# One score product per step in the last third of a fused routing-attention and feed-forward kernel, with the stores of set-aside sums issued a step later

## The chip, the cores and the metric

The kernel runs on one core of one Trainium2 chip. The metric is device time in microseconds (us) of one launch, the median of several executions. A core has five engines that run at the same time and wait for one another through semaphores: PE (matrix products), DVE (vector work), ACT (activations and copies), POOL (more vector work, and some DMA issues) and SP, which here does nothing but issue DMAs. Each engine takes its instructions strictly in program order, so an instruction that waits holds back everything behind it on that engine.

## The reference

Routing attention with 4 batches, 8 heads, 768 tokens and 64 dimensions per head, then a feed-forward block on the (3072 x 512) result:

```
q_assign = argmax(q_n @ c_n.T)            # 16 clusters, per head; k_assign likewise
mask     = q_assign[..., :, None] == k_assign[..., None, :]
scores   = where(mask, scale * q @ k.T, -1e9)
attn     = softmax(scores)                # rows, with + 1e-9 in the sum
x        = concat of heads of attn @ v    # (3072, 512)
h = x @ w_in                              # (3072, 2048)
g = h - tanh(h)
out = g @ w_out                           # (3072, 512)
```

All inputs and the output are float32.

## The kernel before

**Steps.** Attention is worked through in 96 steps. A step is one (pair of heads `n`, half of the queries `half`, third of the keys `s`): it has 2 blocks of 128 keys, 2 heads and 384 queries. There are 16 pairs, 4 for each batch; `HALF` is 12 and `NS` is 3, so the last third of the list is steps 72 to 95 with the pairs 12 to 15 (batch 3). For each step

- `begin` issues the score products (tile `sc`, line 544): 4 matmuls that contract over 64 rows, each head in its own half of PE's rows. ACT then takes the exponential in place (line 566).
- `select` multiplies by the routing mask: 4 DVE instructions (line 576) that compare a row of query codes (`row`, brought from DRAM tensor `q_codes` by `spread`, line 499) with the key's code and write the weights `e`. POOL adds the weights up (`sum`, lines 588 and 592).
- `value` multiplies weights and values (tile `av`, line 601): 4 matmuls that contract over all 128 rows.

The scores of a step are made one step ahead of its values. The weight tiles `e` have two buffers, the score tiles `sc` two, the PSUM tiles of tag `f` three.

**Fills.** Between the products of a step PE is given products of the feed-forward block of the batch before. These come as a list `fill`, whose items each carry a weight; `whole` is the sum of the weights, and step by step items are taken until the share of the weight that is due is spent. For batch 2, which is worked in steps 72 to 95, the list is 56 up products (`pu`, weight 1.3 each) and then 14 down products (`pd`, line 1302): 7 products by Strassen's scheme for each of two blocks of 128 tokens. The function `weight` gives the down products their weights. Each item calls `between`, which issues a slice of the step's other work (`todo`: masks, routing, transposes, checks, stores).

**Runs.** In some steps (where `runs(at)` is true) the kernel does a *run*: it issues the score products of the next three steps one after another, with products of the fill between them, and these are then written in a form that contracts over 64 rows like the scores (`three_in_rows` for the up products, the argument `rows_` for the down products). A down product in this form needs two PSUM tiles, and DVE adds both (two instructions in place of one). The values of the three steps follow later.

**Set-aside blocks.** The third block of 128 tokens of batch 2 (`ASIDE`) is not multiplied in this fill: its seven left operands, and for each the sum of its two halves, are stored to DRAM (`aside`) and multiplied in the tail with batch 3. `set_aside` issues the store of the operand (line 1265), has DVE make the sum into a tile `u` (line 1269; the pool has two buffers), and issues the store of the sum (line 1272). The calls are put on a list, `behind`, which is emptied into `todo` only in a step that is no run and is not followed by one:

```
if not run and not runs(at + 1):
    todo += behind
    behind.clear()
```

With a run in every third step, that is one step in three. All the stores here, the load of `row`, the loads of the factors (`w_in`, line 928) and the loads of weights to be checked (`again`, line 1765) go through SP's queue. Each load of `row` comes after the store of the codes (`q_codes`, line 479), whose source DVE makes (lines 475 and 477).

Of the kernel before, what the change touches and what calls it, by code (L numbers as in the profile page):

```python
# [58 lines left out]
def kernel(  # L59
# [10 lines left out]
    nc = tc.nc  # L70
# [13 lines left out]
    HCH = NCH // 2  # L84
# [95 lines left out]
    def fast():  # L180
# [663 lines left out]
        HF = CF // 2  # L844
        CH = CD // 2
        HM = DM // 2
        HQ, HC = HF // 2, HM // 2
        PRODUCTS = (1, 2, 6, 7, 4, 5, 3)
        SLOT = {which: i for i, which in enumerate(PRODUCTS)}
# [8 lines left out]
        behind = []  # L858
        aside = dram.tile([len(ASIDE), 7, P, HF + HQ, P], F32, name="aside", bufs=1)
# [345 lines left out]
        def strassen_items(b: int):  # L1205
# [31 lines left out]
            aside_ = sum(block[0] == b for block in ASIDE)  # L1237

            def weight(i: int):

                if not aside_:
                    return 3.4
                i = i // HCH * (HCH - aside_) + i % HCH
                return 3.4 if i < 3 else 1.0 if i > 11 else 6.58

            def lower(j: int, which: int, part: int):

# [8 lines left out]
            def set_aside(which: int):  # L1256

                d = [i for i in range(len(ASIDE)) if ASIDE[i][0] == b]
                for i in d:
                    c = slice(ASIDE[i][1] * P, (ASIDE[i][1] + 1) * P)  # L1260
                    quarter_ = {
                        1: (0, 0), 2: (1, 0), 3: (1, 0), 4: (1, 1), 6: (0, 0), 7: (0, 1)
                    }.get(which)
                    t = G[:, :, quarter_[0], quarter_[1], c] if quarter_ else left1[:, :, c]
                    nc.sync.dma_start(aside[i, SLOT[which], :, 0:HF], t)
                    total_ = late_pools["u"].tile([P, 2, TB], F32, name="u")
                    total_ = total_.rearrange("p a n -> p (a n)")[:, 0 : HQ * P]
                    total_ = total_.rearrange("p (a n) -> p a n", n=P)
                    nc.vector.tensor_tensor(  # L1269
                        out=total_, in0=t[:, 0:HQ], in1=t[:, HQ:HF], op=ALU.add  # L1270
                    )
                    nc.sync.dma_start(aside[i, SLOT[which], :, HF : HF + HQ], total_)

            def lower_aside(which: int, part: int):
                for block in ASIDE:
# [3 lines left out]
            def down_product(k_: int, j: int, between, rows_=False):  # L1279
# [66 lines left out]
                if j < 2:  # L1346
                    if k_ == 2:
                        behind.append(lambda: lower_aside(6, j))
                    elif k_ == 4:
                        behind.append(lambda: lower_aside(3, j))  # L1350
                    if (k_, j) in SET_ASIDE:
                        behind.append(lambda: set_aside(SET_ASIDE[k_, j]))
# [306 lines left out]
            if b == B - 1:  # L1659
# [17 lines left out]
                return ups + deep_items()  # L1677
            return ups + [
                (weight(k_ * HCH + j), 2, lambda between, rows_=False, k_=k_, j=j: down_product(k_, j, between, rows_))
                for k_ in range(len(PRODUCTS)) for j in range(HCH) if (b, j) not in ASIDE  # L1680
            ]


        NS = NCH // 2
        HALF = HP * NS
# [161 lines left out]

        def runs(at: int):

            return at > 4 * HALF and at % NS == NS - 1 and at % (2 * HALF) < 2 * HALF - 1  # L1850

        fill, whole, spent, since, over = [], 0.0, 0.0, 0, 1
        for at, (n, half, s) in enumerate(steps):
# [18 lines left out]


            run, chunks = runs(at), []
            if run:
                coming = now + fill
                for _ in range(NS - 1):
                    size = 1 if coming[0][1] == 2 else 3
                    assert all(len(it) == 4 for it in coming[:size]) or size == 1
                    chunks.append(coming[:size])  # L1880
                    coming = coming[size:]
                first_ones = sum(len(it) for it in chunks)
                while len(now) < first_ones + 1:
                    now.append(fill.pop(0))
                    spent += now[-1][0]
                now = now[first_ones:]
            elif runs(at + 1):
                ups_left = sum(len(it) == 4 for it in fill)
                if ups_left < 3 * (NS - 1):
                    for _ in range(ups_left % 3):  # L1890
                        now.append(fill.pop(0))
                        spent += now[-1][0]
# [122 lines left out]
# [3 lines that stand above are left out]
# [317 lines left out]
```

## Time and profile before

| | |
|---|---|
| median of 3 runs | 938.41 us (936.21 to 941.18) |
| profiled execution | 933.44 us |
| its span, first to last instruction | 931.6 us |
| mean granted TensorE clock | 0.995 |
| PE busy | 911.1 us, 98% of the span |
| DVE, POOL, ACT busy | 690.9, 523.6, 295.2 us |
| end of the steps, first product of the tail | 765.35 us after the start |

A row of the timeline has the start in us, how long the merged instructions took, the engine, the source line, the operation, the tile written and the tiles read, the shape and the count; in brackets, how long the engine had been idle before it and which instruction released it. Each float32 matmul shows as two records, so a step's scores are "x8". In a matmul's shape `64*128` means that it contracts over 64 rows, `128*64` that it contracts over 128 rows and makes 64 columns; two such matmuls run side by side. SPq is SP's queue of DMA issues.

### The profile page before, as it was taken

How to read it: one execution, taken by the hardware profiler on the slowest of the kernel's cores; microseconds unless marked ns; L12 is line 12 of the kernel's file. 1: busy time of each engine (PE TensorE's matmuls, PEld its weight loads, DVE VectorE, ACT ScalarE, POOL GpSimd, SP SyncE). 2: the span in 40 equal slices, each digit the busy share in tenths (PEclk: the TensorE clock that was granted, in tenths of full speed). 3: DMA queues.
4: the chain of work that ended last, by engine and by line, in shares of the span. 5: the costliest groups of instructions: out<-in, count | busy, mean ns of one | idle time of the engine just before them, and what ended most of it. 6: DMA issues, size and time to landing. Idle time of an engine off the chain costs nothing.

```text
span 931.6 us, 18750 instructions
## 1 busy us (share of the span) xinstructions
PE 911.1 (98%) x7286; PEld 513.0 (55%) x7286; DVE 690.9 (74%) x1288; ACT 295.2 (32%) x466; POOL 523.6 (56%) x403
## 2 busy tenths in 40 slices
PE   8999999999999999999999999999996999999997
PEld 4434433356653454444666654455563744449997
DVE  7779777986799598666675678766666567867995
ACT  5676653233332323333322213333421211211000
POOL 0236533568878566888664644977773755682000
PEclk9999999999999999999999999999998999999999
DMA  7777584794437974485494666466475446533532
GB/s 170 232 206 182 162 179 130 221 265 135 95 95 238 279 259 117 135 180 183 125 226 149 164 190 149 148 184 166 118 246 178 152 132 190 174 115 139 204 104 84
DMA packets 187439, 158.37 MB, mean 170 GB/s; under 512 B 119200, under 2 KB 161744, under 8 KB 184144
## 3 DMA queue, kind: packets, MB, share of 16 engines
q1 hardware_dynamic: 177696, 134.40, 51.7%
q0 software_dynamic: 6048, 20.98, 6.8%
q10 hardware_dynamic: 3600, 1.74, 0.7%
q8 instruction: 59, 0.97, 0.4%
q14 instruction: 36, 0.29, 0.1%
HBM read 130.33 MB, written 26.75 MB: 169 GB/s over the span
## 4 chain that ended last, share of the span: by engine, by line
PE 87%; DVE 5%; DMA 3%; ACT 1%; issue 1%; POOL 1%; SPq 1%; DVEq 0%; ACTq 0%; POOLq 0%
PE pu L1021 20%; PE sc L544 14%; PE av L601 13%; PE pd L1302 12%; PE pp L1520 9%; PE pu L1012 6%; PE h L787 4%; PE hd L1152 3%; PE o L803 3%; DVE e L576 2%; PE sim L405 1%; DMA row<-q_codes 1%; PE den L674 1%; DMA up_factors<-made 1%; DVE u L1269 1%
## 5 line engine op out<-in xcount | busy, mean ns | idle before, releaser
L592 POOL TENSOR_TENSOR sum<-sum,e 128x768 f32<-128x768 f32 x112 | 206.2, 1841 | 83.8 <-DVE e L576 79.2
L576 DVE SCALAR_TENSOR_TENSOR e<-row,code,sc 128x384 f32<-128x384 bf16 x336 | 183.7, 607 | 63.2 <-ACT sc L566 27.8
L566 ACT ACTIVATE sc<-sc 128x768 f32<-128x768 f32 x168 | 126.5, 793 | 196.5 <-PE sc L544 167.6
L544 PE MATMUL sc<-t,t 64*128 64x384 f32 x768 | 150.1, 506 | 6.8 <-DVE e L576 6.5
L601 PE MATMUL av<-e,vals 128*64 128x384 f32 x768 | 143.7, 494 | 0.0
L1021 PE MATMUL pu<-xT,w_in 128*64 128x384 f32 (+1 forms) x864 | 130.6, 440 | 0.0
L1215 POOL TENSOR_TENSOR G<-G,th 128x768 f32<-128x768 f32 (+1 forms) x51 | 88.0, 1747 | 43.9 <-ACT th L1213 43.8
L1302 PE MATMUL pd<-w_in,G 128*64 128x256 f32 (+1 forms) x960 | 110.5, 381 | 0.2 <-DVE c L1318 0.2
L544 PEld LDWEIGHTS sc<-t,t 64*128 64x128 f32 x768 | 70.3, 187 | 72.7 <-issue 35.8
L1302 PEld LDWEIGHTS pd<-w_in,G 128*64 128x64 f32 (+1 forms) x960 | 81.3, 158 | 30.8 <-issue 5.8
L1021 PEld LDWEIGHTS pu<-xT,w_in 128*64 128x64 f32 x864 | 61.7, 137 | 60.4 <-issue 49.4
L601 PEld LDWEIGHTS av<-e,vals 128*64 128x64 f32 x768 | 51.6, 136 | 75.8 <-issue 68.7
L588 POOL TENSOR_TENSOR sum<-e 128x768 f32<-128x768 f32 x28 | 51.8, 1851 | 72.7 <-DVE e L576 59.7
L1213 ACT ACTIVATE th<-G 128x768 f32<-128x768 f32 (+1 forms) x51 | 39.3, 805 | 109.0 <-DVE G L1006 75.3
L1021 PE MATMUL pu<-diff,w_in 128*64 128x384 f32 x400 | 71.6, 488 | 0.4 <-DVE u L1006 0.4
L803 PE MATMUL o<-w_out,g 128*64 128x512 f32 x256 | 57.4, 593 | 0.0
L1012 PE MATMUL pu<-diff,w_in 64*128 64x384 f32 x176 | 49.6, 482 | 0.0
L1021 PEld LDWEIGHTS pu<-diff,w_in 128*64 128x64 f32 x400 | 28.9, 137 | 35.3 <-issue 27.0
L1012 PE MATMUL pu<-xT,w_in 64*128 64x384 f32 x160 | 48.3, 482 | 0.0
L638 ACT COPY xT<-av 128x384 f32<-128x384 f32 x32 | 15.3, 479 | 94.8 <-PE av L601 94.7
L787 PE MATMUL h<-xT,w_in 128*64 128x384 f32 x256 | 42.8, 486 | 0.0
L1006 DVE TENSOR_TENSOR G<-pu,u 128x384 f32<-128x384 f32 x72 | 38.6, 550 | 5.2 <-PE pu L1021 3.1
(283 smaller groups left out, 1290.7 us busy)
## 6 DMA issues: line engine op xcount, KB each, us to landing
w_in<-up_factors SPq DMA_DIRECT2D x32, 896.0 KB
w_in<-down_factors SPq DMA_DIRECT2D x25, 1024.0 KB
again<-in_moe_w_in_dram SPq DMA_DIRECT2D x32, 256.0 KB
again<-in_moe_w_out_dram SPq DMA_DIRECT2D x32, 256.0 KB
vals<-in_v_dram SPq DMA_DIRECT2D x32, 192.0 KB
raw<-in_moe_w_in_dram POOLq DMA_DIRECT2D x12, 512.0 KB, 4.4
row<-q_codes SPq DMA_DIRECT2D x29, 192.0 KB
raw<-in_moe_w_out_dram POOLq DMA_DIRECT2D x10, 512.0 KB, 4.6
```

What stands on the lines that cost most here:

```text
L544: nc.tensor.matmul(sc[i][:, h, 0:TB], lhsT=turned[n, 1][r].rearrange("p a n -> p (a n)")[:, j * P : (j + 1) * P], rhs=turned[n, 0][r, half ...
L566: nc.scalar.activation(out=out, in_=sc[i][:, :, 0:TB], func=ACT.Exp, scale=SCALE)
L576: nc.vector.scalar_tensor_tensor(out=e[:, h].rearrange("p (j n) -> p j n", n=P), in0=rows[n, half][:, h], scalar=(codes[n][:, h, 1, j : j ...
L592: nc.gpsimd.tensor_tensor(out=s, in0=s, in1=pair[i], op=ALU.add)
L601: nc.tensor.matmul(avs[n, half][h * D : h * D + D], lhsT=vals[n][:, h, j], rhs=e[i][:, h], start=(j == 0), stop=(j == NCH - 1),)
L787: nc.tensor.matmul(h[r], lhsT=w_in[i][:, c, o * P : (o + 1) * P][:, r], rhs=xT[c][:, half], start=(c == 0), stop=(c == CD - 1),)
L803: nc.tensor.matmul(acc[sub][r], lhsT=gs[f % HF][:, f // HF, sub * P : (sub + 1) * P][:, r], rhs=w_out[f // FQ][:, f % FQ], start=(f == seq ...
L1012: return nc.tensor.matmul(ps, lhsT=streams[base + i][r, c, k_], rhs=right[c][r], start=start, stop=stop)
L1021: nc.tensor.matmul(ps[r], lhsT=streams[base + i][:, c, k_, r], rhs=right[c], start=(c == 0), stop=(c == CH - 1),)
L1215: nc.gpsimd.tensor_tensor(out=t, in0=t, in1=th, op=ALU.subtract)
L1302: nc.tensor.matmul(out_, lhsT=w, rhs=x, start=(i == 0), stop=(i == HF - 1))
L1520: nc.tensor.matmul(ps[r], lhsT=left[:, i, r], rhs=right[i], start=(i == 0), stop=(i == HQ - 1),)
```

## The change

Three edits. The score runs are confined to steps before 83 (`7 * HALF - 1`): the four at steps 83, 86, 89 and 92 are no longer made, so from there each step has its own scores, and down products keep their form over 128 rows. The weight of a down product of the fill with a set-aside block becomes 4.55 for all, so that the share of the list done in a step is another. And the store of a set-aside sum is put on `behind` instead of being issued at once: it goes out with the next emptying of the list.

```diff
             def weight(i: int):
 
-                if not aside_:
-                    return 3.4
-                i = i // HCH * (HCH - aside_) + i % HCH
-                return 3.4 if i < 3 else 1.0 if i > 11 else 6.58
+                return 4.55 if aside_ else 3.4
...
                     nc.vector.tensor_tensor(
                         out=total_, in0=t[:, 0:HQ], in1=t[:, HQ:HF], op=ALU.add
                     )
-                    nc.sync.dma_start(aside[i, SLOT[which], :, HF : HF + HQ], total_)
+                    behind.append(lambda total_=total_, i=i: nc.sync.dma_start(
+                        aside[i, SLOT[which], :, HF : HF + HQ], total_
+                    ))
...
         def runs(at: int):
 
-            return at > 4 * HALF and at % NS == NS - 1 and at % (2 * HALF) < 2 * HALF - 1
+            return 4 * HALF < at < 7 * HALF - 1 and at % NS == NS - 1 and at % (2 * HALF) < 2 * HALF - 1
```

The three places below are in steps 85 to 93, with the last two pairs of heads. Lines behind the second edit have other numbers in the changed kernel: the down product's 1302 is 1301 there, the set-aside lines 1265, 1269 and 1272 are 1262, 1266 and 1269.

On PE, the scores of the last pair's first three steps (`t_5743` and `t_5686` are that pair's turned keys). A first shape of 128 rows on a `pd` row is the form over 64 rows of contraction with two outputs; 64 is the form over 128. Before, one run:

```order
L674 MATMUL den<-sum,ones 32x384 x4
L544 MATMUL sc<-t_5743,t_5719 128x384 x4
L1302 MATMUL pd<-w_in_137,G 128x256 x16
L544 MATMUL sc<-t_5743,t_5719 128x384 x4
L1302 MATMUL pd<-w_in_137,G 128x256 x16
L544 MATMUL sc<-t_5743,t_5719 128x384 x4
L1302 MATMUL pd<-w_in_136,G 64x256 x16
L601 MATMUL av<-e,vals 64x384 x12
```

and now, steps 89 and 90, which make the scores of 90 and 91:

```order
L544 MATMUL sc<-t_5686,t_5678 128x384 x4
L601 MATMUL av<-e,vals 64x384 x4
L1301 MATMUL pd<-w_in_138,G 64x256 x16
L674 MATMUL den<-sum,ones 32x384 x4
L1301 MATMUL pd<-w_in_137,G 64x256 x16
L544 MATMUL sc<-t_5686,t_5678 128x384 x4
L601 MATMUL av<-e,vals 64x384 x4
L1301 MATMUL pd<-w_in_137,G 64x256 x16
```

The three scores stood together with down products in their own form between them, and three values followed in one block; now a step's scores, the values of the step before and one or two down products alternate, and PE goes from one form to the other and back in each step.

On SP, the last pair's codes and the stores of set-aside operands. Before:

```order
L479 DMA q_codes<-qc 4x32x32
L1265 DMA aside<-G 128x8x128
L1272 DMA aside<-u 128x512
L1265 DMA aside<-G 128x8x128
L1272 DMA aside<-u 128x512
L1265 DMA aside<-G 128x8x128
L1272 DMA aside<-u 128x512
L1765 DMA again<-in_q_dram 128x384 x2
L499 DMA row<-q_codes 128x768
```

and now:

```order
L479 DMA q_codes<-qc 4x32x32
L1269 DMA aside<-u 128x512 x2
L1262 DMA aside<-G 128x8x128
L499 DMA row<-q_codes 128x768
L928 DMA w_in_136<-down_factors 128x2048
L1262 DMA aside<-G 128x8x128
L1269 DMA aside<-u 128x512
```

Three pairs of stores and two loads stood between the codes and the `row` that is made of them; now two stores of sums made in the step before and one of an operand do.

On DVE, the same place. Before:

```order
L576 SCALAR_TENSOR_TENSOR e<-row,code,sc 128x384 x4
L475 CAST listed_codes<-code 128x12
L477 STREAM_TRANSPOSE qc<-listed_codes 128x32
L1269 TENSOR_TENSOR u<-G 128x512 x3
L1777 TENSOR_REDUCE largest<-again 128x1 x2
L749 TENSOR_TENSOR xT<-xT,den 128x384 x2
L1777 TENSOR_REDUCE largest<-again 128x1 x2
```

and now, in steps 87 and 88:

```order
L576 SCALAR_TENSOR_TENSOR e<-row,code,sc 128x384 x4
L475 CAST listed_codes<-code 128x12
L477 STREAM_TRANSPOSE qc<-listed_codes 128x32
L1317 SCALAR_TENSOR_TENSOR c<-pd,w_in_139 128x256
L1266 TENSOR_TENSOR u<-G 128x512
L1776 TENSOR_REDUCE largest<-again 128x1 x2
L576 SCALAR_TENSOR_TENSOR e<-row,code,sc 128x384 x4
L1266 TENSOR_TENSOR u<-G 128x512
```

Three sums stood in a row ahead of the masks of the last pair; now one stands between two steps' masks, and the two before it were made in step 86.

## The prediction

> **What bounds the kernel now.** I read the page first, for the engine that fills the span.
>
> ```profile
> span 931.6 us, 18750 instructions
> PE 911.1 (98%) x7286; PEld 513.0 (55%) x7286; DVE 690.9 (74%) x1288; ACT 295.2 (32%) x466; POOL 523.6 (56%) x403
> ...
> L592 POOL TENSOR_TENSOR sum<-sum,e 128x768 f32<-128x768 f32 x112 | 206.2, 1841 | 83.8 <-DVE e L576 79.2
> ```
>
> PE is busy 98% of the span, so the time is PE's own work plus what PE waits for. POOL's largest group, the sums of the weights, takes 1.84 us apiece and waits for DVE's masks; that matters below. Second, the waits of PE, longest first (us in total, times, longest):
>
> ```profile
> PE sc L544 <- DVE e L576: 6.5, 1, 6.5
> PE den L647 <- POOL sum L592: 1.9, 1, 1.9
> ```
>
> Both lie in the stretch that the change rewrites. Third, busy time by stretch (us from the start; length, then busy us and counts of the engines, the granted clock, DMA share, GB/s):
>
> ```profile
> 561.38:668.44 107.06, 107.06 (x682) 52.42 (x680) 76.45 (x152) 34.72 (x52) 76.86 (x50) 1.00 0.59 158
> ...
> 705.28:719.55 14.27, 6.63 (x50) 4.11 (x49) 9.01 (x14) 2.47 (x4) 5.22 (x4) 0.91 0.81 240
> 719.55:726.42 6.87, 6.87 (x41) 5.43 (x42) 4.86 (x10) 1.59 (x2) 5.75 (x4) 0.70 0.39 145
> ...
> 263.39:343.41 80.02, 80.02 (x547) 37.30 (x546) 67.49 (x99) 24.91 (x38) 57.88 (x47) 1.00 0.77 223
> ```
>
> The up products of the last third (first row) leave PE no idle time. The trouble starts with the down products, 668.44 to 765.35. Fourth, PE's timeline there:
>
> ```profile
> 700.63 4.72 PE L601 MATMUL av<-e,vals 128*64 128x384 f32 x24
> 705.28 0.84 PE L674 MATMUL den<-sum,ones 128*32 128x384 f32 x4
> 707.29 0.84 PE L674 MATMUL den<-sum,ones 128*32 128x384 f32 x4 [1.17 <-POOL sum L592]
> 708.06 1.56 PE L544 MATMUL sc<-t,t 64*128 64x384 f32 x8
> 709.45 3.62 PE L1302 MATMUL pd<-w_in,G 64*128 64x256 f32 x32
> 719.55 2.93 PE L544 MATMUL sc<-t,t 64*128 64x384 f32 x8 [6.48 <-DVE e L576]
> 722.24 4.36 PE L1302 MATMUL pd<-w_in,G 64*128 64x256 f32 x32
> 726.42 1.47 PE L544 MATMUL sc<-t,t 64*128 64x384 f32 x8
> ...
> 731.32 4.72 PE L601 MATMUL av<-e,vals 128*64 128x384 f32 x24
> 735.97 1.56 PE L544 MATMUL sc<-t,t 64*128 64x384 f32 x8
> 737.37 3.62 PE L1302 MATMUL pd<-w_in,G 64*128 64x256 f32 x32
> 740.82 1.46 PE L544 MATMUL sc<-t,t 64*128 64x384 f32 x8
> 742.11 3.62 PE L1302 MATMUL pd<-w_in,S 64*128 64x256 f32 x32
> ...
> 751.10 4.72 PE L601 MATMUL av<-e,vals 128*64 128x384 f32 x24
> 757.75 0.87 PE L647 MATMUL den<-sum,ones 128*64 128x384 f32 x4 [1.93 <-POOL sum L592]
> ```
>
> Starts tell the pace: undisturbed scores take 1.29 us (740.82 to 742.11), a down product in the scores' form 3.45 (737.37 to 740.82). Values have as many records of as many columns as scores, 1.29, so three in a row should take 3.87. Last, the chain of waits into the 6.48 us:
>
> ```profile
> 702.25 2.19 DVE e L576 x4
> 704.44 0.94 DVE listed_codes L475
> ...
> 705.62 2.17 DVE u L1269
> ...
> 707.81 2.62 DMA aside<-u
> ...
> 714.45 3.69 DMA row<-q_codes
> ...
> 718.26 1.15 DVE e L576 x2
> ...
> 719.55 2.93 PE sc L544 x8
> ```
>
> Three set-aside sums come in one lump. The third needs a buffer, so DVE waits for the first one's store (2.62 us); SP waits for each sum before it goes on; the `row` of the last pair leaves only at 714.45, lands 3.69 later, and PE's second scores wait for its masks.
>
> **The change part by part. What the runs' end removes.** Measured group by group against the pace:
> - 709.45 to 719.55 is 10.10 for a product of 3.45: 6.65.
> - After the pause the clock is 0.70 (windows): scores 2.69 (719.55 to 722.24) for 1.39, the product behind 4.18 for 3.45: 1.30 + 0.73 = 2.03.
> - `den` at 705.28 takes 2.78 to the next scores, of which the last 0.77 (707.29 to 708.06) is work that nothing hides: 2.0, the wait for POOL's last sum (its 1.17 and the lost overlap).
> - 751.10 to 757.75 is 6.65 for three values: 2.78. 0.68 of it recurs in the other two blocks: 700.63 to 705.28 and 731.32 to 735.97 are 4.65, less 3.87 and 0.10 for a change of form: 0.68 each, 1.36. The third value there waits for masks that DVE could start only once the first value had freed an `e` buffer.
>
> Together 6.65 + 2.03 + 2.0 + 2.78 + 1.36 = 14.8. In the new order no three masks are bunched, POOL adds a step's weights while PE has a product of the next, and stores of sums no longer stop SP. I count all of it as gone and price separately what comes late next. DVE's second addition for each 64-row down product (0.96 for two, below) goes too, at no gain: PE, not DVE, ends these stretches.
>
> **What it adds on PE.** Each step by itself costs changes of form. The same alternation stands in other parts of this profile:
>
> ```profile
> 263.39 1.56 PE L544 MATMUL sc<-t,t 64*128 64x384 f32 x8
> 264.88 1.51 PE L601 MATMUL av<-e,vals 128*64 128x384 f32 x8
> 266.22 3.62 PE L1152 MATMUL hd<-w_out,g 128*64 128x256 f32 x32
> 269.78 1.56 PE L544 MATMUL sc<-t,t 64*128 64x384 f32 x8
> ```
>
> Scores 1.49, values 1.34, a product of 32 records 3.56: 6.39 in all, against 1.29 + 1.29 + 3.45 = 6.03. An excursion to the scores' form and back so costs 0.35, and a run costs the same 0.35 for three steps (0.10 in, 0.10 at its first scores, 0.15 out). The order has 16 excursions between the fill's start and the tail, 8 before: 8 x 0.35 = 2.8. Bounds: 2.0 (some changes into the 32-column `den` fall away) and 3.5.
>
> [...]
>
> **The weights.** Moving products between steps is worth nothing by itself: PE's list is the same, and 561.38 to 668.44 had no wait. Its worth is that the 14 down products are spread over steps 85 to 95, two in steps 85, 89 and 93 and one in each of the others.
>
> **What is late next.** DVE, with a step of 6.39 as cover:
>
> ```profile
> 705.54 3.91 DVE L1269 TENSOR_TENSOR u<-G 128x512 f32<-128x512 f32 x2
> ...
> 711.13 1.00 DVE L1777 TENSOR_REDUCE largest<-again 128x1 f32<-128x384 f32 x2
> ...
> 712.05 1.02 DVE L749 TENSOR_TENSOR xT<-xT,den 128x384 f32<-128x384 f32 x2
> ...
> 726.62 0.96 DVE L1318 SCALAR_TENSOR_TENSOR w_in<-pd,w_in 128x256 f32<-128x256 f32 x2 [1.16 <-PE pd L1302]
> 727.33 1.50 ACT L566 ACTIVATE sc<-sc 128x768 f32<-128x768 f32 x2 [3.97 <-PE sc L544]
> ```
>
> Scores need two exponentials before the masks; from scores to the end of four masks is about 4.2 (0.9 until ACT starts, 726.42 to 727.33; one exponential, half of 1.50; 2.19 of masks; gaps). The next scores come 2.2 later. I walk the order with these rows, an estimate: step 86 leaves DVE 2.7 into step 87, step 87's masks end at 5.0, codes at 6.1. SP then issues the codes' store and the two sums' stores, and the third sum (its buffer held a step longer by the deferral) can start when the first has landed, 2.62 on: 3.1 into step 88. Sum and check end at 4.8 to 5.6, the masks behind at 7.0 to 7.8, PE wants them at 7.0: 0 to 0.8 lost. I take 0.4. The last `row` leaves SP about 2 into step 88, lands by 6, and is wanted 2 into step 89: 2 us of slack or more. At the end one down product instead of two covers the last division and differences; the PSUM tile that the tail's fifth product needs is freed about 0.5 late, and a wait of POOL for the last sum may stay: 0.3 to 1.5, I take 0.7. In the 80 us from 263.39 each step already has its own scores, like the one quoted, with DVE busy 67.49 of 80.02 and PE 80.02: the pattern itself needs no wait.
>
> **The sum.** 14.8 - 2.8 - 0.4 - 0.7 = 10.9. The profiled execution took 933.44 (span 931.6), 0.5% under the median; I carry the difference in us: 938.41 - 10.9 = 927.5. [...]
>
> **Rivals.**
> - *The late row stays.* The deferral holds both `u` buffers until the next step; if the codes' store reaches DRAM late, the third sum, the masks behind it and the last `row` slip as before. For it: 2.62 and 3.69 are single rows under heavy traffic (240 GB/s). Against: the 2 us of slack. The pause and the slow clock stay, 8.7 of the 14.8: gain 2.2 to 3, 935.8.
> - *DVE becomes the bound* (the other side). If what DVE has queued in a step exceeds 6.39, every step waits. Masks 2.19, sum 1.55 to 2.31, check 1.00, addition 0.48, scaling 1.02 are 6.2 to 7.0 when all meet in one step; by the order they meet in one or two, and from the first down product to the tail some 64 us of DVE (40 masks, 7 sums, 14 additions, 6 checks, then scalings, divisions and differences) stand in 83 of PE. It decides from about 7.5 in each of 11 steps, where 11 x 1.1 eats the 12.0 won; at 8.0 it is 17.6 lost, 944.0.
> - *POOL's sums stay late.* If POOL is backlogged at both `den`, 2.0 + 2.1 come back: gain 6.8, 931.6. For it: 76.86 of 107.06 busy ahead. Against: a step's sums are two of 1.8 us and their cover is a product and a value, 4.8.
>
> **How the numbers follow.** Forecast 0.75 (its own range 924.5 to 930.5: the bounds of the forms, 0.7 each way, of the new waits, 1.1 down and 1.2 up, and 1.5 for scatter of medians of 936.21 to 941.18); POOL late 0.11; late row 0.09; DVE bound 0.05. What can be told from no change is about 0.5%, 4.7 us: faster means under 933.7. The forecast is faster, POOL's rival nearly always, the late row is within it, DVE's bound mostly slower: faster 0.84, same 0.12, slower 0.04. The range goes from 924 to 933, which leaves out the late row, DVE's bound and a little of each tail.
>
> **What would show it.** Right: no wait of PE over 1 us between 668 and the tail, clock 1.00 throughout, the tail's first product near 755, 10 to 12 earlier, scores 1.49 and values 1.34 in each step, `row` issued within 3 us of the codes. Wrong: PE scores waiting for `e` again with a DMA (`aside<-u` or `row`) behind DVE; or small waits for `e` in most steps, with DVE above 95% there; or `den` still waiting for POOL; or a new wait at the tail's first products larger than 1.5.

## The result, and the profile after

| | before | after |
|---|---|---|
| median of the paired runs | 937.31 us (933.21 to 941.18, 4 runs) | 922.81 us (922.68 to 923.00, 4 runs) |
| profiled execution | 933.44 us | 922.68 us |
| its span | 931.6 us | 920.8 us |
| its mean granted clock | 0.995 | 0.999 |

The changed kernel takes 0.9846 of the time before, 95% interval 0.9803 to 0.9890. That is 1.2 us below the range of the prediction: the direction was right, the forecast of 927.5 was 4.7 too high. Yet the two profiled executions differ by 931.6 - 920.8 = 10.8 us, where the sum said 10.9. Both have to be explained: why the sum came out, and why the medians (14.5 apart) did not follow it.

The page of the changed kernel first. PE's busy time fell by 3.0 us and the span by 10.8, so 7.8 of it is idle time that has gone:

```profile
span 920.8 us, 18740 instructions
PE 908.1 (99%) x7286; PEld 498.5 (54%) x7286; DVE 692.9 (75%) x1280; ACT 295.2 (32%) x466; POOL 523.6 (57%) x403
```

PE's waits (us in total, times, longest). The 6.5 us at the scores are down to two small waits, and no row of the view has `den` waiting for POOL:

```profile
...
PE sc L544 <- DVE e L576: 1.1, 2, 0.8
...
```

Busy time by stretch (length, then busy us and counts of the engines, granted clock, DMA share, GB/s). The clock is 1.00. From 697 to the tail PE is idle for 0.9 us, all of it before 705; there DVE is busy 7.95 of 8.00:

```profile
697.00:705.00 8.00, 7.10 (x54) 3.68 (x52) 7.95 (x10) 1.68 (x3) 5.25 (x4) 1.00 0.92 279
705.00:754.00 49.00, 49.00 (x394) 27.59 (x392) 30.97 (x51) 10.31 (x16) 35.20 (x27) 1.00 0.55 172
```

PE's timeline: the first scores of the stretch, an undisturbed step, step 88, and the first products of the tail.

```profile
670.06 0.92 PE L544 MATMUL sc<-t,t 64*128 64x384 f32 x4
671.33 0.92 PE L544 MATMUL sc<-t,t 64*128 64x384 f32 x4 [0.35 <-DVE e L576]
672.17 1.51 PE L601 MATMUL av<-e,vals 128*64 128x384 f32 x8
...
694.23 1.56 PE L544 MATMUL sc<-t,t 64*128 64x384 f32 x8
695.72 1.51 PE L601 MATMUL av<-e,vals 128*64 128x384 f32 x8
697.06 3.62 PE L1301 MATMUL pd<-w_in,G 128*64 128x256 f32 x32
701.45 1.97 PE L544 MATMUL sc<-t,t 64*128 64x384 f32 x8 [0.77 <-DVE e L576]
703.35 1.51 PE L601 MATMUL av<-e,vals 128*64 128x384 f32 x8
...
753.94 2.75 PE L1021 MATMUL pu<-xT,w_in 128*64 128x384 f32 x16
756.94 2.80 PE L1021 MATMUL pu<-xT,w_in 128*64 128x384 f32 x16 [0.25 <-DVE c L1317]
```

Scores take 1.49 (694.23 to 695.72), values 1.34 (695.72 to 697.06), as forecast. In step 88 the product takes 4.39 (697.06 to 701.45) in place of 3.55 and the scores 1.90 in place of 1.49: 1.25 lost. The chain of waits into it tells why (start, length, what):

```profile
691.95 1.97 DVE listed_codes L475
...
694.18 0.57 SPq L479
...
694.80 2.23 DMA aside<-u
...
697.05 0.04 DVE u L1266
697.09 2.17 issue
699.26 1.00 DVE largest L1776 x2
700.26 1.06 DVE e L576 x2
...
701.45 0.92 PE sc L544 x4
```

The codes leave at 694.18, the first set-aside store behind them; DVE's third sum can start only when it has landed, 2.23 on, and takes 2.2 itself (697.05 to 699.26); the check and the masks come behind. This is the new wait of the prediction, at the place that it named. The `row` left SP at 696.34, 2.2 behind the codes, where before it had left behind six stores and two loads, 8.8 behind them (705.65 to 714.45).

### The profile page after: what moved, and what is told of

It reads as the page before. It is cut to its first block, busy times and chain, and to the rows that moved or that the text cites. A ratio compares the mean times of both kernels' runs of the same rounds, so it can differ in the third digit from the quotient of the medians.

```text
span 920.8 us, 18740 instructions
## 1 busy us (share of the span) xinstructions
PE 908.1 (99%) x7286; PEld 498.5 (54%) x7286; DVE 692.9 (75%) x1280; ACT 295.2 (32%) x466; POOL 523.6 (57%) x403
## 4 chain that ended last, share of the span: by engine, by line
PE 92%; DVE 4%; ACT 1%; issue 1%; DMA 1%; POOL 0%; SPq 0%; DVEq 0%; ACTq 0%
PE pu L1021 20%; PE sc L544 15%; PE av L601 14%; PE pd L1301 12%; PE pp L1519 9%; PE o L803 6%; PE pu L1012 5%; PE h L787 5%; PE hd L1152 3%; PE sim L405 1%; DVE e L576 1%; PE den L674 1%; PE den L647 1%; PE den L627 1%; POOL G L1215 0%
## 5 line engine op out<-in xcount | busy, mean ns | idle before, releaser
L1021 PE MATMUL pu<-xT,w_in 128*64 128x384 f32 (+1 forms) x872 | 132.5, 441 | 0.2 <-DVE c L1317 0.2
L544 PEld LDWEIGHTS sc<-t,t 64*128 64x128 f32 x768 | 67.8, 186 | 70.5 <-issue 32.7
L1301 PEld LDWEIGHTS pd<-w_in,G 128*64 128x64 f32 (+1 forms) x960 | 74.0, 147 | 35.6 <-issue 6.3
L601 PEld LDWEIGHTS av<-e,vals 128*64 128x64 f32 x768 | 49.7, 136 | 77.3 <-issue 73.5
L1021 PE MATMUL pu<-diff,w_in 128*64 128x384 f32 x416 | 74.1, 488 | 0.5 <-DVE u L1006 0.4
L1012 PE MATMUL pu<-diff,w_in 64*128 64x384 f32 x160 | 45.8, 482 | 0.0
L1012 PE MATMUL pu<-xT,w_in 64*128 64x384 f32 x152 | 45.1, 482 | 0.0
```

Of the source, the lines that this page charges most:

```text
L544: nc.tensor.matmul(sc[i][:, h, 0:TB], lhsT=turned[n, 1][r].rearrange("p a n -> p (a n)")[:, j * P : (j + 1) * P], rhs=turned[n, 0][r, half ...
L601: nc.tensor.matmul(avs[n, half][h * D : h * D + D], lhsT=vals[n][:, h, j], rhs=e[i][:, h], start=(j == 0), stop=(j == NCH - 1),)
L1012: return nc.tensor.matmul(ps, lhsT=streams[base + i][r, c, k_], rhs=right[c][r], start=start, stop=stop)
L1021: nc.tensor.matmul(ps[r], lhsT=streams[base + i][:, c, k_, r], rhs=right[c], start=(c == 0), stop=(c == CH - 1),)
L1301: nc.tensor.matmul(out_, lhsT=w, rhs=x, start=(i == 0), stop=(i == HF - 1))
```

## The experiments

Eighteen kernels ran, in several groups; each group had runs of the kernel before on the same chip beside it. All medians of before below are from such groups: 935.6, 935.17, 936.02, 935.94 and 935.09.

### The kernel before, once more

No edit.

> The kernel before, once more, to see what differs between its executions. Theory A (the scatter of before, 933 to 941, is the wait for the last pair's row of codes in the step of the three lumped sums, which is longer in most executions than in the one shown): this execution's profile has the same PE rows everywhere but there; the scores behind that product wait 6 to 15 us, and time minus that wait is constant within 1 us. Rival (the scatter is spread over the whole program, a slower chip or slower transfers): the wait stays near 6.5 and the difference is found in the first two thirds. Median 935 to 940 either way, spread of several us.

936.59 us (933.76 to 938.79, 10 runs), ratio 1.0012 (0.9998 to 1.0026). The profiled execution has a span of 935.4, 3.8 more than the one that the prediction read. PE's waits are the same, the long one with 6.4 us too, but for one of 0.78 at an early `den`; so the long wait is not what differs. About 0.9 of the 3.8 arises before 56 us, 0.6 more by 477, 0.5 behind the long wait, and 1.7 here, at the two down products behind the second wait (PE's timeline, then a stretch of the windows):

```profile
759.72 0.91 PE L647 MATMUL den<-sum,ones 128*64 128x384 f32 x4 [1.93 <-POOL sum L592]
```

```profile
760.41:769.00 8.59, 8.59 (x66) 5.39 (x64) 6.76 (x11) 0.49 (x1) 3.27 (x4) 0.80 0.63 200
```

In the execution that the prediction read, the same products took 6.91 at clock 1.00:

```profile
758.44:765.35 6.91, 6.91 (x66) 4.60 (x64) 5.08 (x8) 0.49 (x1) 2.72 (x3) 1.00 0.62 183
```

So a wait of 1.93 us is followed by a slow clock in one execution and not in another. A profile of one execution cannot show that.

### Each edit by itself, and in pairs

The runs confined, old weights, store at once (only this edit):

```diff
-            return at > 4 * HALF and at % NS == NS - 1 and at % (2 * HALF) < 2 * HALF - 1
+            return 4 * HALF < at < 7 * HALF - 1 and at % NS == NS - 1 and at % (2 * HALF) < 2 * HALF - 1
```

> Before, with the third edit alone: no score runs in the last third, weights and stores as before. Theory A (the runs make the lump): nearly all of the gain, 922 to 926, and a spread under 1 us between executions. Rival B (the deferred stores are what freed SP): the wait for the row stays in part, 928 to 935. Rival C (the even weights are what gives each step its cover): steps without a down product show waits for masks, 925 to 930.

931.59 us (929.57 to 932.50, 6 runs), ratio 0.9956 (0.9937 to 0.9976). PE's waits:

```profile
PE sc L544 <- DVE e L576: 5.2, 3, 3.1
PE den L647 <- POOL sum L592: 2.6, 1, 2.6
```

This is a third of the gain: with the old weights three waits for masks stay, and the one for POOL's last sum has grown from 1.9 to 2.6.

The runs and the weights, without the deferral:

```diff
-                return 3.4 if i < 3 else 1.0 if i > 11 else 6.58
+                return 4.55 if aside_ else 3.4
...
+            return 4 * HALF < at < 7 * HALF - 1 and at % NS == NS - 1 and at % (2 * HALF) < 2 * HALF - 1
```

> The changed kernel with the stores of the sums issued at once again (first and third edit). Theory A: with one sum a step SP waits for it at no cost; the third sum no longer waits 2.3 us for a store issued a step late, and the scores behind it no longer 0.8: 921.5 to 923, 0 to 1.3 faster than the changed kernel. Rival B: SP held by each sum, the row late, 925 to 930.

923.58 us (923.38 to 923.88, 4 runs), ratio 0.9879 (0.9859 to 0.9899). Beside the 922.81 of the changed kernel the deferral would be worth 0.8 us, beside the 925.17 of its second sample (below) it would cost 1.6: by the medians it cannot be told from nothing. The profile says more:

```profile
PE h L787 <- DVE xT L767: 1.4, 1, 1.4
...
PE sc L544 <- DVE e L576: 0.4, 1, 0.4
```

Without the deferral step 88 has no wait; the 0.4 is at the first scores of the stretch. The third sum (696.36) stands right behind the codes and waits for no store, and the `row` (699.62) leaves 3.2 behind the codes (696.47) in place of 2.2, still early enough. So the wait of step 88, 1.25 us, is the deferral's doing, and no row of PE in this stretch shows a gain from it. The 1.4 at `h` belongs to a chain that is treated below.

The runs and the deferral, with the old weights (the first two lines of that diff left as before):

> The changed kernel with the old weights (second and third edit). Theory A: PE's list is the same, the down products stand less evenly; a step with none has 2.8 us between its scores and the next against some 4.2 that masks need, so each such step costs up to 1.5: 923 to 927. Rival C (weights matter most): 928 or more.

932.07 us (929.04 to 933.20, 10 runs), ratio 0.9955 (0.9935 to 0.9976). Its longest wait stands behind the routing of the last pair:

```profile
688.27 3.62 PE L1304 MATMUL pd<-w_in,G 128*64 128x256 f32 x32
695.02 2.70 PE L544 MATMUL sc<-t,t 64*128 64x384 f32 x8 [3.13 <-DVE e L576]
697.66 2.27 PE L601 MATMUL av<-e,vals 128*64 128x384 f32 x8
```

One down product stands in the step of the routing, where the new weights put two, and DVE has five operations of the routing, then two sums of 0.68 and 3.44 us ahead of the masks. Behind the wait the scores take 2.64. `den` waits 2.6 for POOL here too.

The weights alone, with the runs kept:

> Before, with the first edit alone: even weights, runs and stores as before. The even weights were worth 9 us on top of the other two edits. Theory A (that worth comes only with single steps: the routing then stands in a step of two products, and no step is without cover): alone, with three sums still lumped between runs, the long wait of the scores stays, 931 to 937. Rival (the even weights help whatever else is done): 925 to 929.

942.50 us (941.62 to 943.34, 4 runs), ratio 1.0086 (1.0067 to 1.0106): slower, and above both ranges expected. The long wait grew, and a load came late:

```profile
PE sc L544 <- DVE e L576: 13.3, 2, 11.7
PE pu L1021 <- DMA w_in<-up_factors: 3.9, 1, 3.9
```

In the chain into the 11.7, two sums wait for stores, 2.55 and 4.00, and only then comes the `row`:

```profile
703.26 2.55 DMA aside<-u
...
707.06 4.00 DMA aside<-u
...
715.06 3.71 DMA row<-q_codes
```

Together: against a before of about 935.5, runs off gives 4, the weights alone cost 7, both give 12. Moving products is worth nothing or less by itself; where each step has its own scores, it is worth some 8 us. The deferral alone on the kernel before was not tried: by the code, three sums in a lump cannot be made in two tiles when their stores are issued behind them.

### Where the long wait came from

The kernel before with small products of PE in its two waits, 26 and 8:

```diff
+                        if at == 7 * HALF + 5 and i == 0:
+                            keep_busy(26)
...
+                        if n == len(pairs) - 1 and half == 1:
+                            keep_busy(8)
```

> Before, with 26 products of the identity with itself (0.22 us each, 5.7 in all) put on PE into its 6.5 us wait for the masks and 8 (1.75) into its 1.9 us wait for the last sum; they compute nothing that is used. Theory A (the scatter and 4 to 8 us of the time are the half-rate clock that follows these two pauses, longer in some executions than in the one profiled): clock 0.998 or more, 929 to 931.5, spread under 1.5. Rival (the transfers behind the wait differ from run to run): 934 to 937 and a spread of several us; the products can only add.

935.87 us (933.41 to 938.07, 10 runs), ratio 1.0003 (0.9989 to 1.0018): no gain, though the mean clock was 0.996 to 0.999 where the kernel before has 0.992 to 0.995 on the same chip. The profiled execution is the slowest of the ten; in it the masks came later and PE still waited:

```profile
715.39 6.07 PE L330 MATMUL busy<-ident 128*128 128x128 f32 x52
723.54 2.70 PE L550 MATMUL sc<-t,t 64*128 64x384 f32 x8 [2.08 <-DVE e L582]
726.00 4.44 PE L1308 MATMUL pd<-w_in,G 64*128 64x256 f32 x32
```

Behind these 2.08 us the scores still took 2.46 (723.54 to 726.00) for 1.39 and the clock from 722 to 730 is 0.79, so this execution did not get rid of the slow clock. (Behind the 6.48 us wait of the execution that the prediction read, the clock is 0.50 from 719.55 to 723.00 and 1.00 from 724.00 on.) The second wait was covered, and the clock stayed at 1.00 behind it. Three executions have a mean clock of 0.996 and took 935.98 to 938.07; but the seven at 0.998 or 0.999 lie 3.5 apart (933.41 to 936.88), so the clock is not all of the scatter.

The set-aside sums by turns in tiles of two pools, so that the third waits for no store, in the changed kernel and then in the kernel before:

```diff
-                    total_ = late_pools["u"].tile([P, 2, TB], F32, name="u")
+                    pool_ = ("u", "th")[deep.setdefault("sums", 0) % 2]
+                    deep["sums"] += 1
+                    total_ = late_pools[pool_].tile([P, 2, TB], F32, name=pool_)
```

> The changed kernel with the sums' tiles taken in turn from two pools, so that four are free instead of two. The third sum then needs no store to land (2.3 us of waiting on DVE), and the scores behind it no longer wait 0.8: theory A 921.3 to 921.8, 1.0 to 1.5 faster than the changed kernel's 922.8. Rival (another wait takes its place, since the masks then wait for the row): no change.

923.77 us (920.63 to 925.12, 4 runs), ratio 0.9877 (0.9849 to 0.9904). In its profile the wait of step 88 is gone, but 2.8 us were lost before 80 us, a place that no edit touched. PE there:

```profile
...
70.28 1.51 PE L787 MATMUL h<-xT,w_in 128*64 128x384 f32 x8 [0.71 <-DVE xT L749]
73.36 6.03 PE L787 MATMUL h<-xT,w_in 128*64 128x384 f32 x36 [1.57 <-DVE xT L767]
```

and DVE, which waits for a load of divisors:

```profile
69.66 0.56 DVE L749 TENSOR_TENSOR xT<-xT,den 128x384 f32<-128x384 f32 x1 [4.20 <-DMA den<-back]
```

That load is the last of a chain through DRAM: sums stored, loaded in another layout, inverted, stored (`back`), loaded again (`den`). SP issued the last store at 56.52 and the load that waits for it at 62.38, 5.9 later. In the shown profile of the changed kernel the store left at 56.21 and the load at 59.59, 3.4 later, and PE did not wait.

> Before, with the sums' tiles from two pools in turn. Theory A (the chain into the long wait has the third sum waiting for the first one's store, 1.1 to 2.6 us, and SP behind it): the row leaves 1 to 2 us earlier, the scores wait 4.5 to 5.5 instead of 6.5, the slow clock behind stays: 1 to 2.5 us faster than before. Rival (SP is held by the sums themselves, which wait in a row of 2 us each, not by the store): within 0.5 us of before.

936.12 us (932.64 to 937.88, 9 runs; a tenth took 1904.27, twice as long, and is left out), ratio 1.0005 (0.9987 to 1.0022), and its scores still waited 6.3. So in the kernel before the third sum's wait for its store is not what sets the long wait. The third sum started at once, but the last two took 1.7 each (709.53 to 712.88), so that the three filled 5.51 us (707.37 to 712.88), where with the wait they had filled 5.59; and the `row` left 8.8 behind the codes as before (707.48 to 716.27). The sums themselves hold SP, with the check and the two loads behind them.

### The changed kernel again, and pauses put into it

> The changed kernel again, unedited, with the kernel before on the same chip. The question is why the medians differ by 14.5 us (937.31 to 922.81) where the two profiled executions differ by 10.8. Theory A: the executions of before scatter (932.6 to 942) because their pauses of PE have an aftermath of varying size, and a kernel without pauses does not scatter: 922.5 to 923.5, all executions within 1 us. Theory B: the scatter stands in the first 75 us, where the load of the divisors that scale the attention output (den, read from DRAM) lands up to 3 us late in some executions, and is common to both kernels: 922.5 to 926, median 923.5 to 924, so that the difference of large samples is 11 to 12. Both can hold in part; then the spread here is that of B and the rest of the spread of before is that of A.

925.17 us (921.99 to 927.41, 6 runs), before 936.02 (932.95 to 940.92, 26 runs) on the same chip, ratio 0.9888 (0.9863 to 0.9913). This is wider than either theory expected. So the changed kernel scatters too, and the four runs of the result, within 0.3 us, were a lucky draw. In this pair of samples the medians differ by 10.85 us.

A pause of 29 copies put into the changed kernel at step 89; in the last of the four kernels with a pause, a second one of 9 copies follows at step 94. `products` is 0 here:

```diff
+            for _ in range(1 + products):
+                nc.tensor.matmul(ps, lhsT=pad, rhs=ident, start=True, stop=True)
+            for _ in range(copies):
+                nc.scalar.copy(out=pad, in_=ident[:, 0:D])
+            nc.tensor.matmul(ps, lhsT=pad, rhs=ident, start=True, stop=True)
```

> The changed kernel with an idle wait of PE put in at step 89, ahead of the scores: a small product reads a scratch tile, ACT then copies into that tile 29 times (about 0.22 us each, 6.4 us), and a second small product waits for the copies. Nothing else is added but one copy at the start. Theory A (a pause costs its length and a slow clock behind it): 922.8 + 6.4 + 2.0 = 931.2, mean clock 0.996, granted clock about 0.7 over the 7 us behind the pause, executions more scattered than the filled twin's. Rival (the clock behind the pause is not the pause's doing): 929.2, equal to the twin. [...]

934.19 us (932.51 to 939.86, 12 runs), ratio 0.9988 (0.9971 to 1.0005). The pause came out longer than meant, 8.07. PE behind it, and the granted clock of that stretch:

```profile
710.09 0.69 PE L336 MATMUL mark<-ident,pad 128*64 128x128 f32 x2 [8.07 <-ACT pad L335]
710.71 2.93 PE L556 MATMUL sc<-t,t 64*128 64x384 f32 x8
713.57 1.97 PE L613 MATMUL av<-e,vals 128*64 128x384 f32 x8
715.38 3.62 PE L1313 MATMUL pd<-w_in,G 128*64 128x256 f32 x32
```

```profile
710.71:718.92 8.21, 8.21 (x49) 4.10 (x48) 1.14 (x2) 2.07 (x3) 0.00 (x0) 0.77 0.00 1
```

Scores 2.86 for 1.49 and values 1.81 for 1.34: 1.84 us lost behind the pause. The profiles of the next kernel and of the one with two pauses have the same pause of 8.11; they lost 2.23 and 1.37 behind it, counted in the same way.

> The same kernel as the one with the idle pause, but with 26 more small products on PE in front of the wait (52 records, about 6 us), so that PE is busy over nearly all of the pause. Theory A: 922.8 + 6.4 = 929.2, clock 0.999, 2 us faster than the idle twin, the executions as little scattered as the changed kernel's. Rival: the same time as the idle twin.

939.43 us (938.65 to 943.46, 9 runs), ratio 1.0046 (1.0028 to 1.0064). This kernel, with 26 products, did not test the theory: the products read the tile that the copies write, so the copies waited for all of them, and the whole idle pause of 8.11 came behind 6.06 us of products. With a tile of their own, and 33 products:

```diff
+            for _ in range(products):
+                nc.tensor.matmul(ps, lhsT=ident[:, 0:D], rhs=ident, start=True, stop=True)
```

> The filled twin of the kernel with the idle pause, mended: the first twin's products read the tile that ACT copies into, so the copies waited for them and the pause came behind the products (6.06 us of products, then the whole 8.1 us of idle wait). Here 33 small products (about 7.7 us) that read another tile stand between the mark and the wait, beside the 29 copies (8.0 us). Theory A: the clock stays at 1.00, the scores behind it take 1.49 and the values 1.34, and the time is 1.8 us below the idle twin's 934.19 (in whose profile scores took 2.86 and values 1.81 behind the pause): 932.4. Rival (the slow clock is not the idle time's doing): 934.2, with the same slow rows.

932.25 us (929.54 to 934.07, 12 runs), ratio 0.9953 (0.9935 to 0.9972); clock 0.998 to 1.000 in each execution, where the idle twin had 0.992 to 0.995. PE, and the stretch behind:

```profile
711.23 0.43 PE L337 MATMUL mark<-ident,pad 128*64 128x128 f32 x2 [0.86 <-ACT pad L336]
711.59 1.56 PE L557 MATMUL sc<-t,t 64*128 64x384 f32 x8
713.08 1.51 PE L614 MATMUL av<-e,vals 128*64 128x384 f32 x8
```

```profile
711.59:719.00 7.41, 7.41 (x59) 3.83 (x60) 2.04 (x5) 2.06 (x4) 0.00 (x0) 1.00 0.01 3
```

The twins have the same copies and nearly the same length of pause; the filled one is 1.94 us faster by the medians (they ran in two groups, whose kernels before had 936.02 and 935.94), and its scores are not slowed. The rows say the same without the scatter of other places: from the end of the pause to `den` the idle twin takes 8.21 (710.71 to 718.92), the filled one 6.39 (711.59 to 717.98). The slow clock, 0.77 behind the idle pause and 1.00 behind the filled one, is the idle time's doing.

> The kernel with the idle pause and a second idle wait of 9 copies (about 2 us) five steps later, as the kernel before has its wait of the divisors (den) some 35 us behind its wait of the scores. In one profiled execution of before that second wait of 1.9 us was followed by a clock of 0.80 over 8.6 us (1.7 us lost), in another it was not. Theory A: the time of the idle pause + 2.0 to 3.7 with executions spread over at least 1.7 us, 933.2 to 934.9; rival (a wait of 2 us does nothing to the clock): + 2.0 in every execution, 933.2.

937.67 us (935.09 to 939.56, 12 runs), ratio 1.0016 (0.9999 to 1.0032): 3.5 over the single pause. The second pause was 2.56 us, 3.3 with its two products. Three executions had a mean clock of 0.995 and took 935.09 to 935.25, the other nine had 0.991 to 0.993 and took 936.8 to 939.6, their median 937.8. The profiled execution is one of the three, and its clock behind the second pause is 1.00. So a short wait now costs its length and now, by the medians of the two groups, 2.7 us more; that the slow clock of the nine stands behind the second pause was not profiled here, only in the kernel before (above, 0.80). The 110 executions of before in these groups divide alike: 64 with a clock of 0.994 or more have a median of 934.9, 46 below it 936.9.

### Where the changed kernel scatters

The wait at `h` stands in the profiles of three kernels so far: 1.6 us behind a first wait of 0.7 in that with four tiles, 1.4 in that without the deferral, 1.6 in that with the filled pause. The second chain of divisors moved up, on SP and by one step on DVE:

```diff
-                        (0, total), (1, compact), (2 + more, invert), (3 + more, spread_out),
+                        (0, total), (1, compact), (2 + (more and n == 0), invert), (3 + (more and n == 0), spread_out),
...
-            for it in later.pop(at, []):
+            for it in sorted(later.pop(at, []), key=lambda it: it[0] if at == 6 else 0):
```

> The changed kernel with the second chain of divisors of the first batch moved up: on SP the loads of its sums (each, other) go ahead of the loads of the first chain's divisors instead of behind them, and DVE's addition and reciprocal stand one step earlier; nothing else moves, and PE's list is the same. In the profiles this chain through DRAM (store back, then load den) ends 62 to 70 us after the start, and DVE wants it at 65; where it is late, PE waits up to 2.8 us at the products h. Theory B (the scatter of the changed kernel's executions, 922.0 to 927.4, is this chain): all executions within 921.5 to 923.5, median 922.5 to 923. Rival (the scatter is elsewhere, such as code or transfers at the start, or the work around the kernel): 922 to 927 as before, median 924 to 925.

926.30 us (924.34 to 928.46, 6 runs), ratio 0.9884 (0.9856 to 0.9912). No gain: the late wait at `h` was gone, but DVE's addition now stood ahead of the sum that PE needs, and waited for its load:

```profile
53.88 0.82 PE L627 MATMUL den<-sum,ones 128*32 128x384 f32 x2 [2.12 <-DVE sum L617]
```

The scores behind it took 2.41 (55.30 to 57.71), at a clock of 0.71.

> The kernel before with the same two edits. Its executions lie from 932.6 to 942. Theory B alone: 932.5 to 934. Theory B with A (its short wait of the divisors in the tail, 1.9 us, leaves a slow clock behind it in some executions and not in others): two groups, about 932.5 to 934 at a clock of 0.994 to 0.995 and 934.5 to 936 at 0.991 to 0.992, median 934 to 935, about 1.5 below the kernel before. Rival (neither): as the kernel before, median 935.8.

937.87 us (935.14 to 940.66, 12 runs), ratio 1.0006 (0.9987 to 1.0025), with the same new wait (2.5). Its executions do fall into two groups, five at a clock of 0.994 or 0.995 within 935.1 to 935.9 and seven at 0.989 to 0.993 from 937.75 up.

> The changed kernel with the divisors' chain moved up and with the set-aside sums made by turns in tiles of two pools, so that the third sum of a step waits for no store. If both act as their traces say: 1.25 us (the wait of step 88) below the changed kernel with the early divisors, 921.3 to 921.8. Rival: equal to it.

925.72 us (923.99 to 926.85, 6 runs), ratio 0.9873 (0.9846 to 0.9900), again with the new wait (3.0).

The same early loads, with DVE's addition behind the sum (the first change of the diff above left out):

```diff
-            todo += listed
+            todo = listed + todo if at == 8 else todo + listed
```

> The changed kernel with the early divisors, as in the run of that name, but with DVE's addition and reciprocal behind the sum that PE waits for instead of ahead of it. In the earlier run the load that they need landed at 52.6, DVE waited for it, and PE lost 2.1 us at den and 1.1 in slow scores behind it; the chain's later part was early enough (no wait at the products h). Theory B (the scatter of the changed kernel is this chain): 921.5 to 924, median 922.5 to 923, neither wait in the profile. Rival (the scatter is elsewhere): 922 to 927, median about 925, as the changed kernel.

924.10 us (923.55 to 925.08, 6 runs), ratio 0.9877 (0.9854 to 0.9901). Neither wait is in its profile. The executions lie 1.5 apart, those of the changed kernel 5.4; the median fell by 1.1, less than forecast and within the interval. The rows show that the chain costs up to 2.8 in some profiles and nothing in others, so it is a part of the scatter; six executions each do not show how large a part.

> The same with the set-aside sums by turns in tiles of two pools, so that the third sum of a step waits for no store: 1.25 us less than the run before it if the wait of step 88 is worth its length, 921.3 to 921.8; equal to it if another wait comes in its place.

922.23 us (921.68 to 923.71, 6 runs), ratio 0.9860 (0.9836 to 0.9884), 1.9 below the kernel with the chain alone, on the same chip (1.25 was expected). Step 88 has no wait left:

```profile
697.79 3.62 PE L1303 MATMUL pd<-w_in,G 128*64 128x256 f32 x32
701.34 1.56 PE L544 MATMUL sc<-t,t 64*128 64x384 f32 x8
```

It has the lowest median of the long samples, 2.9 under the changed kernel's second sample; by the ratios (0.9860 and 0.9888) the intervals still overlap.

## Why the prediction was right or wrong

**What bounds, and what the end of the runs removes: right, and 0.9 too small.** What made up the 14.8 us has gone: no long wait at the scores, none at `den`, the clock at 1.00, no block of three values. That the 2.03 behind the pause belong to the pause is shown by the idle and the filled twin (1.4 to 2.2 in three profiles, for a pause of 8). One loss was overlooked. In the kernel before two steps' scores and two products stood here:

```profile
686.64 0.59 PE L1302 MATMUL pd<-w_in,G 64*128 64x256 f32 x2
687.48 3.47 PE L1302 MATMUL pd<-w_in,G 64*128 64x256 f32 x29 [0.25 <-DVE c L1318]
...
697.13 3.67 PE L1302 MATMUL pd<-w_in,G 128*64 128x256 f32 x32
```

They take 10.49 (686.64 to 697.13), where the prediction's pace gives 2 x 3.45 + 2 x 1.29 = 9.48 and 0.10 for the change of form behind them: 0.9 lost.

**Forms: 2.8 forecast, about 2.7.** The changed kernel's tail began at 753.94, 11.41 earlier; 0.32 of that stood already at the first up product of the last third (561.06 for 561.38). That leaves 11.09 for the stretch, and with 1.87 of new waits 14.8 + 0.9 - 11.09 - 1.87 = 2.74. This is a remainder; the price of a step is measured: from 687.85 to 694.23, scores to scores, an undisturbed step takes 6.38, where the prediction had 6.39.

**New waits: 0.4 forecast, 1.87.** Step 88 lost 1.25 for 0 to 0.8, by the mechanism named. Two rows were longer than the walk took them: the cast of the codes took 1.97 for about 1, and the third sum 2.2 for 0.7 to 1.5, though the prediction's own rival has sums of up to 2.31. Another 0.62 went at the first scores of the stretch (670.06 to 672.17, 2.11 for 1.49), which the walk through the order did not reach. With four tiles, and without the deferral, step 88 has no wait: a sum that is held in one of two tiles until the next step is its cause.

**The end: 0.7 forecast, 0.6** (11.41 less the 10.8 of the spans). It went where it was put, to the tail's first products and not to POOL: the first 32 records take 5.94 (753.94 to 759.88, with a wait of 0.25 for DVE at 756.94) where in the kernel before they took 5.40 (765.35 to 770.75).

**The sum** so came out by errors that cancel: 14.8 + 0.9 - 2.7 - 1.9 - 0.6, with the 0.3 of the start, is 10.8.

**The weights: incomplete.** "Moving products between steps is worth nothing by itself" does not hold: alone it costs 7 us. The prediction names what they are for, the spread of the products over steps 85 to 95, but it has no price for the order that the old weights would have left, and does not make the new ones a condition of the 14.8. Without them the gain is 4, not 12.

**The step that failed: "I carry the difference in us: 938.41 - 10.9 = 927.5".** The difference belonged to executions; it was hung on a median of three that stood 2.7 above the median of 110 later executions (935.76), with 1.5 in the range for scatter. The changed kernel's own four runs then lay 2.4 below its second sample. In that second pair of samples, 936.02 - 925.17 is 10.85. From 935.76 to 925.17 it is 10.6, 0.3 less than the sum; so the 4.7 are 2.65 + 2.36 - 0.3. What the single profile could not show: two sources of scatter, the slow clock that sometimes follows the 1.93 us wait of the kernel before (1.7 us there), and the divisors' chain through DRAM (up to 2.8 us in a profile), which both kernels have. The prediction read an execution in which neither had struck, 933.44, and set its difference against a median with both. Not settled: how the remaining scatter divides, since the kernel with PE busy in the pauses still lies 4.7 apart, and why four executions of the changed kernel agreed within 0.3.

**Rivals.** The late row did not stay (2.2 behind the codes). POOL's sums were not late in the changed kernel; with the old weights `den` does wait 2.6 for POOL. DVE was no bound: 30.97 of 49.00 us behind step 88, full only in that one step.

## What to carry to other kernels

A gain that is worked out from one profiled execution is a difference between executions. Hang it on the median of a sample that is large enough (935.76 - 10.9 = 924.9, beside 925.17 in the changed kernel's second sample), and before choosing a range ask how far a median of three or four lies from it and which waits could strike by chance. Hung on the profiled execution, 933.44, the 10.9 would have met the four runs of the result (922.5 for 922.81), but by the luck of that draw. PE's pause of 8 us had a price beyond its length (1.4 to 2.2 us in three profiles), and the filling of a pause by other work only shows this if nothing that ends the pause waits for the filling. Taking away a bunched order paid here only where the work was also spread to cover what each step needs; either edit alone gave a third of the gain (4 us of 12) or a loss (7 us).

## What was not expected of the hardware

In these profiles a wait of 2 us sits on an edge: clock 0.80 over the 8.6 us behind a wait of 1.93 in one execution, 1.00 in another, and in the kernel with two pauses three executions of twelve without the loss. The profiles of all kernels here say how wide the edge is. Take each wait of PE of 0.6 us or more (behind the first 20 us of the program) and the granted clock in the 8 us behind it. Behind the 22 waits of 0.65 to 1.88 us it is 1.00 every time. Of the 10 waits of 1.93 to 2.59 us six have 0.79 to 0.81 behind them and four 1.00. Behind the 12 waits of 2.96 us and more it is 0.64 to 0.79 every time. The same DRAM round trip of a small store and its load took 3.4 us from issue to issue in one execution and 5.9 in another, of kernels that have the same code there. And one vector operation on the same shape, the sum of two halves, took 0.68 us in one place and 3.44 in the next; during the longer one POOL made two sums of its own (689.76 to 692.27), but no run here shows whether that is the cause.
